# The fourth window's last head pair through a DMA, and the whole order searched anew

## The chip, the cores and the metric

The kernel runs on one core of one Trainium2 chip. The metric is the device time of one execution in microseconds (us); lower is better. The time given for the kernel before is the median of three runs.

## The reference

For 4 batches, 8 heads, 768 tokens and a head dimension of 48, a gated linear attention keeps a 48x48 state per head, and a feed-forward network (FFN) with an ELU between its two matrices follows:

```python
for t in range(S):
    state = alpha[:, :, t, :, None] * state + np.einsum('bhd,bhe->bhde', k[:, :, t], v[:, :, t])
    y[:, :, t] = np.einsum('bhd,bhde->bhe', q[:, :, t], state)
...
x = attn_out.transpose(0, 2, 1, 3).reshape(B * S, H * D)      # 3072 x 384
h = x @ w_in                                                  # 384 x 2048
g = np.where(h > 0.0, h, np.exp(np.minimum(h, 0.0)) - 1.0)
return g @ w_out                                              # 2048 x 384
```

The two weight matrices come as 64-bit floats. The result is fp32.

## The kernel before

**Windows.** Each batch is cut into 6 windows (spans) of 128 tokens, 24 windows in all. A window holds all 8 heads as 4 head pairs; the FFN's input has 3 x 128 rows, so the first three pairs lie in it as they are computed and the fourth has to be spread over the free rows of the other three. The recurrence is done in chunks of 64 tokens by matmuls. Steps are written as tokens, name.window:

- L loads a window's k, q and alpha in one transfer (LA and LB: alpha alone, and k or q alone, for the first two windows); LV loads v. All input transfers, weight transfers and most outputs are issued by SP's queue, in order.
- SC is the scan of alpha on VectorE (DVE, L300), LN and EX are Ln and Exp on ScalarE (ACT, L312 and L318), KA, KB and KC scale k (L326, L331, L336; KA and KB on DVE or GpSimd (POOL), by the tables KAV and KBV), SQ scales q (L354, L357, table SQV), PC is a check sum on ACT (L341).
- TP transposes k on TensorE (PE, L379) and KN copies it out on ACT (L409); for later windows T does both on DVE (L389).
- S makes the scores (L444, L428), MK masks them on DVE (L461, L456), U, UA, UB, UC carry the state (L491, L473; L508 to L541).
- Y (L552 for windows 0 to 4, L557 behind) makes the window's output, XH copies it to the FFN's input xt as the high part (L620, L621), XL makes the low part (L643 and L647 on DVE; XP and a copy on ACT for windows 0 to 2).

**The fourth head pair.** For windows below DIRECT, YL makes that pair's output alone (L552, tile yl), Y3 copies it (L594), and the first matmuls of Y spread it over the free rows by a selection matrix (L606, 6 matmuls, 12 records). For the other windows Y makes all four pairs, XH and XL write the fourth pair's high and low parts into a tile of its own, and XD moves them into xt by two DMAs on SP (L654):

```python
for a in range(2):
    nc.sync.dma_start(out=x[64 * a + D:64 * a + 64]..., in_=y3[64 * a:64 * a + D]...)
```

**Weights.** F loads one piece of 768 KB. KW (ACT, L687), DA (L703) and DB (L708, both DVE) make fp32 words of it, WH (ACT, L735) the high part and WL (L755, DVE or POOL by the table WLV) the low part. LC, CA and CB check the weights. F, KW, DA, DB, WH and WL of all 16 pieces end at about 100 us.

**FFN.** There are 9 blocks: three of 256 tokens (2 windows each, 8 steps j), six of 384 (3 windows, 16 steps). A.b.j makes h in a PSUM bank (L787), RA, RB (ACT, L796, L801) and RC (DVE, L807) the ELU, GH (ACT, L813) and GL (L820, DVE or POOL by the table GQ) its high and low parts, O.b.j multiplies by the second matrix (L836), Z copies the result out (L846) and sends it (L849). RC also frees h's bank. The tiles r, gh, gl and ot come from a ring of 11 buffers.

**The order.** A string of some 1,640 tokens (ORDER) gives one order for the whole program; each engine takes its instructions in that order and waits for what it needs. BANKS and SLOTS are strings that give each PSUM tile its bank and each ring tile its buffer. X.n tokens and WARM put dummy matmuls on PE (L209, tiles xf and wp).

Of the kernel before, what the change touches and what calls it, by code (L numbers as in the profile page):

```python
# [61 lines left out]
YL.1 Y3.1 XP.0 Y.1 WH.2 XL.0 WH.0 F.6 MK.2 YL.2 KA.3 KB.3 KC.3 TP.3 WL.0 XH.1 KN.3 XP.1 XL.1 S.3 WL.2 F.4 KW.2 F.3
DA.2 Y3.2 LV.3 A.0.0 KW.1.1 RA.0.0 DA.1.1 F.7 F.1 DB.2 WH.6 WL.6 UB.2 DB.1.1 Y.2 XH.2 U.3 L.5 MK.3 F.5 UC.2 UA.3 PC.3
A.0.1 YL.3 WH.4 WL.4 KW.1.0 DA.1.0 RB.0.0 RC.0.0 DB.1.0 SC.5 RA.0.1 GH.0.0 UB.3 GL.0.0 L.4 RB.0.1 Y3.3 F.8 WH.1 A.0.3
RA.0.3 WL.1 WH.3 WL.3 XP.2 XL.2 F.10 RB.0.3 RC.0.1 Y.3 XH.3 LV.7 RC.0.3 UC.3 XL.3 KW.3 A.0.2 DA.3 SC.4 LN.5 A.1.1 DB.3
RA.0.2 RB.0.2 RA.1.1 EX.5 KA.5 O.0.0 RB.1.1 A.1.0 KW.4 RC.0.2 RC.1.1 RA.1.0 RB.1.0 GH.0.1 GL.0.1 GH.0.2 LN.4 F.12 DA.4
DB.4 WH.10 RC.1.0 GH.1.0 LC.1 A.1.3 KB.5 GL.1.0 WH.7 WH.8 WL.7 GH.1.1 F.9 GL.0.2 GL.1.1 A.1.2 O.0.1 RA.1.2 RB.1.2
WL.10 EX.4 O.1.0 CA.1 RC.1.2 KA.4 WH.5 WL.8 O.1.1 GH.1.2 WL.5 RA.1.3 RB.1.3 GL.1.2 A.1.5 RC.1.3 GH.0.3 F.14 ZV.6 KW.6
DA.6 CB.1 F.11 A.0.4 O.1.2 RA.0.4 RB.0.4 A.0.5 RA.1.5 O.0.2 KB.4 DB.6 WH.14 GL.0.3 SQ.4 KC.4 S.4 WH.12 RB.1.5 RA.0.5
RC.0.4 L.6 KC.5 RC.1.5 DA.5 GH.0.4 KW.5 LV.6 MK.4 TP.4 RB.0.5 GH.1.5 RC.0.5 KN.4 TP.5 KN.5 LC.3 DB.5 GH.1.3 O.0.3 PC.4  # L70
SQ.5 CA.3 LV.5 U.5 WH.9 WL.12 S.5 MK.5.1 MK.5.0 A.0.6 WH.11 WL.11 CB.3 RA.0.6 GL.1.3 O.1.3 LV.4 U.4 RB.0.6 RC.0.6 PC.5
# [1026 lines left out]
```

## Time and profile before

| | |
|---|---|
| median of three runs (464.18 to 464.94) | 464.34 us |
| the profiled execution, whole | 465.35 us |
| its span, first to last instruction | 463.5 us |
| mean granted clock of PE | 0.997 |
| PE, DVE, ACT, POOL busy | 98%, 75%, 71%, 46% |

The profile is of one execution. A stretch of the span gives each engine's busy time in us and its count of instructions, PE's granted clock, the share of the DMA engines and what they moved. A line of the timeline gives start, duration, engine, line, operation, and in brackets how long the engine stood still before it and what released it; "x18" merges instructions that follow each other. Matmuls are pipelined, so a merged line is read by start times.

### The profile page before, as it was taken

Reading aid. Unit: us, or ns where it says so; the run is one execution under the profiler, and the core shown is the slowest. Engines: PE = TensorE matmul, PEld = TensorE weight load, DVE = VectorE, ACT = ScalarE, POOL = GpSimd, SP = SyncE. Lnnn points to the kernel's source line nnn. Section 1 sums busy time; section 2 is a strip of 40 time slices with the busy share of each in tenths; the row PEclk is TensorE's granted clock in tenths of the full one; section 3 lists DMA queues with packets and bytes.
Section 4 is the critical chain, followed back from the end, with each engine's and each line's share of the span. In section 5 each row is a group of like instructions: output and inputs, shape, how many; then the busy total and the mean of one; then the engine's idle time right before and its main releaser. Section 6 shows DMA issues by size and latency. Waiting matters only on the chain.

```text
span 463.5 us, 12462 instructions
## 1 busy us (share of the span) xinstructions
PE 456.1 (98%) x4948; PEld 440.3 (95%) x4948; DVE 349.7 (75%) x756; ACT 327.6 (71%) x741; POOL 214.2 (46%) x185
## 2 busy tenths in 40 slices
...
GB/s 256 415 411 286 306 103 159 150 157 104 90 236 10 172 116 178 123 49 138 47 176 139 126 66 179 155 70 154 78 120 35 121 45 52 34 35 85 35 4 57
DMA packets 23715, 61.10 MB, mean 132 GB/s; under 512 B 3040, under 2 KB 10720, under 8 KB 23648
## 3 DMA queue, kind: packets, MB, share of 16 engines
...
q10 hardware_dynamic: 432, 0.59, 0.3%
...
HBM read 53.52 MB, written 4.72 MB: 126 GB/s over the span
## 4 chain that ended last, share of the span: by engine, by line
PE 88%; ACT 5%; DVE 4%; issue 1%; DMA 1%; POOL 0%; DVEq 0%; ACTq 0%; POOLq 0%
PE h L787 38%; PE o L836 38%; PE y L557 4%; PE q L428 2%; PE q L473 2%; PE wp L209 1%; PE y L552 1%; ACT w L735 1%; DVE raw L703 1%; DMA out_dram<-ot 1%; DVE wm L708 1%; ACT gh L813 1%; ACT r L801 1%; ACT r L796 1%; PE y L606 1%
## 5 line engine op out<-in xcount | busy, mean ns | idle before, releaser
L787 PE MATMUL h<-xt,w 128*128 128x384 f32 (+1 forms) x1296 | 200.1, 310 | 0.3 <-DVE r L807 0.3
L787 PEld LDWEIGHTS h<-xt,w 128*128 128x128 f32 x1296 | 190.8, 190 | 1.5 <-DVE r L807 0.4
L836 PE MATMUL o<-w,gh 128*128 128x384 f32 x768 | 188.4, 327 | 0.0
L820 POOL TENSOR_TENSOR gl<-r,gh 128x384 fp32r<-128x384 f32 (+1 forms) x90 | 106.4, 1189 | 158.7 <-ACT gh L813 104.9
L836 PEld LDWEIGHTS o<-w,gh 128*128 128x128 f32 x768 | 134.0, 189 | 0.5
L836 PE MATMUL o<-w,gl 128*128 128x384 f32 x384 | 125.3, 326 | 0.2 <-POOL gl L820 0.2
L796 ACT ACTIVATE r<-h 128x384 f32<-128x384 f32 (+1 forms) x120 | 60.5, 510 | 55.8 <-PE h L787 49.3
L389 DVE STREAM_TRANSPOSE kn<-qka 32x128 f32<-32x128 f32 x256 | 77.5, 303 | 4.2
L807 DVE SCALAR_TENSOR_TENSOR r<-r,h 128x384 f32<-128x384 f32 (+1 forms) x90 | 51.0, 577 | 38.0 <-ACT r L801 31.4
L836 PEld LDWEIGHTS o<-w,gl 128*128 128x128 f32 x384 | 72.6, 189 | 0.6 <-POOL gl L820 0.5
L801 ACT ACTIVATE r<-r 128x384 f32<-128x384 f32 (+1 forms) x120 | 64.1, 543 | 2.0
L813 ACT CAST gh<-r 128x384 fp32r<-128x384 f32 (+1 forms) x90 | 46.4, 528 | 18.6 <-DVE r L807 16.1
L357 POOL TENSOR_TENSOR st<-qka,P 64x512 f32<-64x512 f32 x34 | 43.0, 1265 | 17.4 <-DVE P L300 16.1
L456 DVE TENSOR_TENSOR st<-q,mask 64x256 f32<-64x256 f32 x76 | 32.1, 422 | 9.2 <-PE q L428 6.0
L326 POOL TENSOR_TENSOR qka<-qka,R 128x512 f32<-128x512 f32 x16 | 21.1, 1316 | 29.9 <-ACT R L318 27.8
L807 DVE SCALAR_TENSOR_TENSOR h<-r,h 128x384 f32<-128x384 f32 (+1 forms) x30 | 17.5, 589 | 21.0 <-ACT r L801 20.5
L300 DVE TENSOR_TENSOR_SCAN P<-qka,first 128x516 f32<-128x516 f32 (+1 forms) x25 | 31.0, 1244 | 0.5 <-DMA qka<-in_qka_dram 0.2
L820 DVE TENSOR_TENSOR gl<-h,gh 128x384 fp32r<-128x384 f32 (+1 forms) x30 | 17.3, 582 | 18.2 <-ACT gh L813 7.7
L726 ACT ACTIVATE ck<-ck,lim 128x384 f32<-128x384 int32 x32 | 25.5, 795 | 0.6
L721 ACT ACTIVATE ck<-ck,lim 128x384 int32<-128x384 int8 x32 | 25.3, 792 | 0.0
L312 ACT ACTIVATE R<-P 128x512 f32<-128x512 f32 (+1 forms) x25 | 15.4, 615 | 11.4 <-DVE P L300 11.3
L813 ACT CAST gh<-h 128x384 fp32r<-128x384 f32 (+1 forms) x30 | 14.8, 497 | 8.8 <-DVE h L807 7.2
...
## 6 DMA issues: line engine op xcount, KB each, us to landing
qka<-in_qka_dram SPq DMA_DIRECT2D x18, 770.0 KB, 5.5
...
raw<-in_wgt_dram SPq DMA_DIRECT2D x16, 767.6 KB, 10.5
...
xt<-y SPq DMA_DIRECT2D x40, 48.0 KB, 2.8
```

What stands on the lines that cost most here:

```text
L300: nc.vector.tensor_tensor_scan(out=P[:, n].rearrange("p n w -> p (n w)"), data0=t[:, 2 * NP * W + n.start * AW:2 * NP * W + n.stop * AW], ...
L357: eng(SQV, i).tensor_tensor(out=st[r, a], in0=d["q"][r], in1=pw(i)[r], op=ALU.mult)
L389: nc.vector.transpose(out=kn[32 * t:32 * t + 32, :, 32 * g:32 * g + 32], in_=d["kt"][32 * g:32 * g + 32, :, 32 * t:32 * t + 32])
L456: nc.vector.tensor_tensor(out=d["st"][r, a, :, c * C:(c + 1) * C], in0=d["s4"][a][o], in1=mask[o].unsqueeze(1).broadcast_to([64, NP, C]), ...
L726: nc.scalar.activation(out=t[:, :, 1].bitcast(F32), in_=t[:, :, 0], func=AF.Square, bias=lim[:, 1:2], accum_out=chk_w[:, f:f + 1])
L787: nc.tensor.matmul(h[:, y, :], lhsT=t[:, wi, ws], rhs=x[:, c, xi].rearrange("p (a x) -> p x a", a=2), start=(y == 0 and k == 0), stop=(k = ...
L796: nc.scalar.activation(out=r, in_=d["h"], func=AF.Relu, scale=-1.0)
L801: nc.scalar.activation(out=d["r"], in_=d["r"], func=AF.Exp, scale=-1.0)
L807: nc.vector.scalar_tensor_tensor(out=d["g"], in0=d["r"], scalar=-1.0, in1=d["h"], op0=ALU.add, op1=ALU.max)
L813: nc.scalar.copy(out=gh, in_=d["g"])
L820: q.tensor_tensor(out=gl, in0=d["g"], in1=d["gh"].bitcast(F32), op=ALU.subtract)
L836: nc.tensor.matmul(o[:, 0:DM], lhsT=gt[:, y, ms], rhs=t[:, wi, f * DM:f * DM + DM].rearrange("p (a x) -> p x a", a=2), start=(u == 0 and y ...
```

## The change

DIRECT goes from 4 to 3, so window 3 takes the way of the later windows. WARM goes from 17 to 14, and the fillers from X.4.1, X.4.2, X.2.0 to X.2.1, X.2.2, X.2.0. The five engine tables, ORDER, BANKS and SLOTS are replaced; apart from YL.3, Y3.3, XD.3 and the X tokens ORDER holds the same tokens. The functions are as they were.

```diff
-DIRECT = 4
+DIRECT = 3
...
-WARM = 17
+WARM = 14
...
-WLV, KAV, KBV, SQV = (0, 2, 7, 8, 10, 11, 13, 15),  \
-    (0, 1, 2, 3, 6, 7, 14, 22),  \
-    (0, 1, 2, 3, 4, 7, 11, 22, 23),  \
-    (0, 1, 18, 19)
+WLV, KAV, KBV, SQV = (0, 3, 5, 11, 14),  \
+    (0, 1, 3, 4, 5, 16, 18, 21, 23),  \
+    (0, 1, 2, 5, 6, 16, 17, 20, 21, 22, 23),  \
+    (0, 1, 3, 19)
...
-LA.0.0 SC.0.0 LN.0.0 EX.0.0 LA.0.1 SC.0.1 LB.0.0 LN.0.1 KA.0.0 LV.0.0 KB.0.0 EX.0.1 KC.0.0 TP.0.0 KA.0.1 KB.0.1 KC.0.1
...
+LA.0.0 SC.0.0 X.2.1 X.2.2 LA.0.1 SC.0.1 LN.0.0 EX.0.0 LN.0.1 LA.1 EX.0.1 SC.1 LN.1 LB.0.0 KA.0.1 KA.0.0 KB.0.0 LB.0.1
...
```

GQ holds 90 pairs before and after; 15 of them are exchanged.

DVE at the start of the program, before. The input of window 0 is qka_128, that of window 1 qka_129; L300 is the scan:

```order
L300 SCALAR_TENSOR_TENSOR P<-qka_128,first 128x258 x2
L326 TENSOR_TENSOR qka_128<-qka_128,R 128x256
L331 TENSOR_TENSOR R<-P,R 128x256
L336 SCALAR_TENSOR_TENSOR qka_128<-R,qka_128 128x256
...
L300 SCALAR_TENSOR_TENSOR P<-qka_129,first 128x516
L354 TENSOR_TENSOR st<-qka_129,P 128x512
L354 TENSOR_TENSOR st<-qka_128,P 128x512
L326 TENSOR_TENSOR qka_129<-qka_129,R 128x512
```

The same engine and place after, with window 0 in qka_125 and window 1 in qka_126:

```order
L300 SCALAR_TENSOR_TENSOR P<-qka_125,first 128x258 x2
L300 SCALAR_TENSOR_TENSOR P<-qka_126,first 128x516
L326 TENSOR_TENSOR qka_125<-qka_125,R 128x256 x2
L331 TENSOR_TENSOR R<-P,R 128x256 x2
L336 SCALAR_TENSOR_TENSOR qka_125<-R,qka_125 128x256 x2
L354 TENSOR_TENSOR st<-qka_125,P 128x512
L326 TENSOR_TENSOR qka_126<-qka_126,R 128x512
L331 TENSOR_TENSOR R<-P,R 128x512
```

The scan of window 1 has moved ahead of window 0's KA, KB and KC, and only one SQ stands ahead of window 1's KA.

SP's queue behind the first weight loads, before. L676 are weight loads; L260 loads qka_130 for window 5 and qka_129 for window 4:

```order
L676 DMA raw_508<-in_wgt_dram 128x6141
L676 DMA raw_478<-in_wgt_dram 128x6141
L260 DMA qka_130<-in_qka_dram 128x1540
L676 DMA raw_508<-in_wgt_dram 128x6141
L260 DMA qka_129<-in_qka_dram 128x1540
L676 DMA raw_622<-in_wgt_dram 128x6141 x2
L287 DMA vs_115<-in_vv_dram 64x768
```

After; window 5 is loaded into qka_127, window 4 into qka_126, and L654 is XD.3, which waits for XL.3 on DVE:

```order
L676 DMA raw_587<-in_wgt_dram 128x6141
L260 DMA qka_127<-in_qka_dram 128x1540
L676 DMA raw_597<-in_wgt_dram 128x6141
L676 DMA raw_587<-in_wgt_dram 128x6141
L676 DMA raw_597<-in_wgt_dram 128x6141
L654 DMA xt<-y_636 16x6x128 x2
L260 DMA qka_126<-in_qka_dram 128x1540
L716 DMA ck<-in_wgt_dram 128x768
```

The load for window 4 has moved from ahead of two weight loads to behind XD.3.

PE around window 3's output, before; y_620 and sel are the selection matmuls, w_428 and w_512 the first FFN matrix:

```order
L787 MATMUL h<-xt,w_428 128x256 x18
L552 MATMUL yl<-st,vs_115 64x64 x8
L787 MATMUL h<-xt,w_512 128x256 x18
L625 MATMUL y<-xt,minus 128x384
L606 MATMUL y<-y_620,sel 64x128 x6
L552 MATMUL y<-st,vs_115 48x64 x24
L787 MATMUL h<-xt,w_512 128x256 x18
```

After, with w_427 and w_509 as that matrix and vs_112 as window 3's v:

```order
L787 MATMUL h<-xt,w_427 128x256 x18
L625 MATMUL y<-xt,minus 128x384
L552 MATMUL y<-st,vs_112 64x64 x32
L787 MATMUL h<-xt,w_509 128x256 x36
L836 MATMUL o<-w_601,gh 128x384 x2
```

The separate yl matmuls and the six selection matmuls are gone from this place, and two steps of A stand between Y.3 and the first O.

## Rows read from the trace of the kernel before

**Rows 1.** The page's busy time, share of the span and instructions by engine.

```profile
PE 456.1 (98%) x4948; PEld 440.3 (95%) x4948; DVE 349.7 (75%) x756; ACT 327.6 (71%) x741; POOL 214.2 (46%) x185
```

**Rows 2.** Stretches: length, busy us (instructions) by engine, clock, DMA share, GB/s.

```profile
0.00:5.00 5.00, 3.93 (x10) 1.45 (x11) 2.98 (x13) 2.45 (x5) 2.82 (x13) 1.00 0.56 160
5.00:10.00 5.00, 5.00 (x23) 2.20 (x21) 4.73 (x9) 2.10 (x7) 0.00 (x0) 1.00 0.97 306
10.00:15.00 5.00, 4.40 (x105) 3.54 (x104) 3.96 (x7) 2.14 (x6) 0.14 (x1) 1.00 1.03 418
...
60.00:70.00 10.00, 10.00 (x102) 9.71 (x102) 9.98 (x9) 9.09 (x14) 9.34 (x6) 1.00 0.45 120
```

**Rows 3.** Timeline of PE, 0 to 30 us: start, us, what, count.

```profile
1.07 6.78 PE L209 MATMUL wp<-wz 128*128 128x512 bf16 x17 [1.07 <-DVE wz L184]
...
7.91 1.03 PE L209 MATMUL xf<-wz 128*128 128x512 bf16 x4
...
13.30 0.66 PE L379 MATMUL tp<-ident,qka 128*128 128x128 f32 x4 [0.60 <-DVE qka L336]
...
27.66 2.27 PE L787 MATMUL h<-xt,w 128*128 128x256 f32 x18
```

**Rows 4.** Timeline of DVE and ACT in the same stretch.

```profile
7.61 1.23 DVE L300 TENSOR_TENSOR_SCAN P<-qka,first 128x516 f32<-128x516 f32 x1
...
9.19 0.59 ACT L409 COPY kn<-tp 128x512 f32<-128x512 f32 x1 [0.75 <-PE tp L379]
...
9.68 0.64 ACT L312 ACTIVATE R<-P 128x512 f32<-128x512 f32 x1
...
11.10 0.69 DVE L326 TENSOR_TENSOR qka<-qka,R 128x512 f32<-128x512 f32 x1 [0.94 <-ACT R L318]
...
17.82 0.69 DVE L336 SCALAR_TENSOR_TENSOR qka<-R,qka 128x512 f32<-128x512 f32 x1
```

**Rows 5.** Timeline at the two late starts of PE behind 28 us.

```profile
78.11 1.16 PE L787 MATMUL h<-xt,w 128*128 128x256 f32 x8 [0.29 <-DVE r L807]
...
315.57 0.48 ACT L846 COPY ot<-o 128x384 f32<-128x384 f32 x1
...
319.89 0.51 ACT L813 CAST gh<-r 128x384 fp32r<-128x384 f32 x1 [0.27 <-DMA out_dram<-ot]
...
321.57 0.43 PE L836 MATMUL o<-w,gl 128*128 128x384 f32 x1 [0.19 <-POOL gl L820]
```

**Rows 6.** Chain that ended last, in order of time: start, us, what.

```profile
23.15 0.87 PE y L606 x12
...
37.84 0.80 PE y L606 x12
```

**Rows 7.** A group of instructions, and DMA issues (KB each, median us to landing).

```profile
L643 DVE TENSOR_TENSOR y<-y,y 128x128 fp32r<-128x128 f32 x20 | 5.7, 286 | 4.2 <-ACT xt L621 4.0
...
qka<-in_qka_dram SPq DMA_DIRECT2D x18, 770.0 KB, 5.5
...
raw<-in_wgt_dram SPq DMA_DIRECT2D x16, 767.6 KB, 10.5
...
xt<-y SPq DMA_DIRECT2D x40, 48.0 KB, 2.8
```

**Rows 8.** Timeline: SP's issues, and two steps of DVE.

```profile
23.55 0.33 SPq L260 DMA_DIRECT2D qka<-in_qka_dram  x1
25.45 2.22 SPq L676 DMA_DIRECT2D raw<-in_wgt_dram  x2
...
41.39 0.55 DVE L647 TENSOR_TENSOR xt<-y,xt 128x384 fp32r<-128x384 f32 x1
...
43.08 1.21 DVE L300 TENSOR_TENSOR_SCAN P<-qka,first 128x516 f32<-128x516 f32 x1
```

**Rows 9.** Timeline of PE where it goes from FFN to window work and back.

```profile
314.08 0.33 PE L836 MATMUL o<-w,gl 128*128 128x384 f32 x1
314.34 0.69 PE L428 MATMUL q<-st,qka 48*64 48x64 f32 x32
...
316.40 4.66 PE L787 MATMUL h<-xt,w 128*128 128x384 f32 x27
```

More of the change, by code (lines that the diff above doesn't have):

```diff
@@ L62 @@
[L62 to L71, printed above, removed]
@@ new lines @@
+O.2.3 SC.10 LN.10 EX.10 LV.10 XD.7 RA.2.6 RB.2.6 KA.11 KB.11 GH.2.5 ZV.12 KC.11 PC.11 O.2.4 T.11.0 T.11.2 RC.2.6
+RA.2.7 T.11.1 RB.2.7 KA.10 KB.10 KC.10 GH.2.6 T.10.3 GL.2.5 T.10.1 XD.8 A.3.0 RA.3.0 RC.2.7 A.3.1 A.3.2 LC.4 CA.4
+GL.2.6 SQ.11 RA.3.2 RB.3.2 RC.3.2 O.2.5 L.12 RB.3.0 RC.3.0 LV.11 T.11.3 T.10.2 GH.2.7 GL.2.7 O.2.6 O.2.7 A.3.3 T.10.0
+SQ.10 GH.3.0 GL.3.0 MK.9.0 CB.4 RA.3.1 RB.3.1 SC.12 U.11 S.11 MK.11.0 S.10 Z.2.0 Z.2.1 LN.12 EX.12 RC.3.1 GH.3.1
+MK.11.1 GH.3.2 U.10 RA.3.3 MK.10.1 MK.10.0 RB.3.3 UA.10 A.3.4 RA.3.4 LC.5 RC.3.3 PC.10 KA.12 A.3.14 RA.3.14 UB.10
@@ new lines @@
+RA.5.5 RB.5.5 O.5.1 T.18.0 RC.5.5 A.5.9 RA.5.9 RB.5.9 LC.14 CA.14 KB.19 KC.19 CB.14 MK.17.0 PC.19 T.19.3 O.5.2 T.19.2
+O.5.3 RA.5.10 T.19.0 A.5.7 RA.5.7 RB.5.7 A.5.13 GL.5.4 RC.5.9 O.5.4 RB.5.10 A.5.8 RC.5.10 LC.15 GH.5.5 GL.5.5 GH.5.9
+GL.5.9 GH.5.6 GL.5.6 O.5.5 O.5.6 RA.5.8 RB.5.8 T.18.2 T.18.1 LV.18 U.18 CA.15 CB.15 S.18 LV.19 UA.18 RC.5.8 GH.5.8
+RC.5.7 T.19.1 GH.5.7 Y.17 XH.17 UB.18 UC.18 A.5.15 GH.5.10 RA.5.15 MK.18.0 L.20 GL.5.7 XL.17 RB.5.15 GL.5.8 O.5.7
+O.5.8 MK.18.1 RA.5.13 RB.5.13 RC.5.13 U.19 SC.20 LN.20 GL.5.10 RC.5.15 S.19 A.5.11 UA.19 GH.5.13 MK.19.1 RA.5.11
```

172 lines of the change are left out of this document (86 added, 86 removed), and 8 rows, old and new, of the table GQ.

## The prediction

> **What bounds the kernel now.** I read the busy shares first, then the stretches, then the instructions of TensorE (PE) in order of time. PE is busy for 98% of the span [rows 1], and in a middle stretch such as 60 to 70 us for all of it [rows 2]. So the span is PE's own work plus the few places where PE stands still. There are three kinds. At the start PE runs dummy matmuls or waits for the first windows: one chain of VectorE (DVE), ScalarE (ACT) and transposes leads to the first FFN matmul at 27.66 us [rows 3, 4]. Behind that, two starts of matmuls are late by more than switching costs: at 78.1 us behind a DVE step that frees an accumulator, and at 321.6 us behind a POOL step [rows 5]. Last comes the output of block 8, which the change leaves as it is. The reader is to see that nothing an engine other than PE saves counts by itself: it counts if it removes PE work, shortens the first 27.7 us, or removes a late start. The reverse holds too: DVE is busy 9.98 us of the 10 from 60 to 70 us [rows 2], so a DVE that falls behind there shows up on PE at once.
>
> The sums go against the profiled execution (span 463.5 us, 1.85 us more as a whole, 465.35). That one is 1.01 us above the median of the runs, 464.34, so I apply the differences to the median. A measurement of this kernel tells about 0.2% from no change, 0.93 us.
>
> **Part 1, the head pair of the fourth window.** With DIRECT at 3, window 3 loses YL, Y3 and the 12 records of selection matmuls at the front of Y: 0.80 us [rows 6]. The state and score matmuls of that pair move from YL into Y, one for one (8 and 24 become 32). PE is dense there, so 0.80 us goes in full: **-0.8 us**. What is added lies off PE: one L643 on DVE (0.29 us, [rows 7]), one accumulator read on ACT, and XD.3, two DMAs of 48 KB. The first FFN matmuls on that block (A.1.3) now wait for XD.3. The 40 transfers of this kind took 2.8 us to land in the median [rows 7], but none of them ran before 93 us, when the queues are emptier. I cost XD.3 at nothing: XL.3 ends at 41.94 us at the latest (as before, [rows 8]), by the following sums near 38, and PE has A.0.2, A.0.3 and O.0.0 between Y.3 and A.1.3, some 6 us of work (18 matmuls of A take 2.2 us, [rows 3]). With ACT's steps between Y.3 and XL.3 that covers 2.8 us and two issues with some 1.5 us to spare. If that cover is gone, the price is the rest of the landing, 0 to 2 us.
>
> **Part 2, the start.** Three warm-up matmuls and four fillers go. In the trace PE runs 17 warm-ups for 6.78 us and four fillers for 1.03 us before the second transpose; that transpose lets ACT make kn at 9.19, and only behind it ACT starts the Ln of window 1 at 9.68, although window 1's scan ended at 8.84 [rows 3, 4]. Exp, KA.1 (11.10) and KC.1 follow, and the transposes of window 1 start at 13.30. Now the scan of window 1 stands before KA on DVE, and Ln and Exp before kn on ACT. The scan waits for LA.1, third in SP's order; the third transfer of before was read at 5.09 or earlier. So: scan 5.1 to 6.3, the six half-width steps 2.1 to 2.6 us, SQ.0 0.65, then KA.1 to KC.1 with the 2.14 us that the trace shows from 11.10 to 13.24. That puts window 1's transposes at 11.2 to 11.8, against 13.30: 1.5 to 2.1 us earlier.
>
> Part of it is given back to the loads. In the first 10 us the queues move 160 and 306 GB/s, behind that 418 at a share of 1.03, which is all they have [rows 2]. DA.0.0 now stands ahead of MK.1 on DVE and needs F.0, with 3.74 MB up to its end: 0.80 + 1.53 MB by 10 us, the rest by 13.4, landed at 14 to 15. Then 0.6 (DA), 0.6 (MK.1), 0.35 (UC.1), 1.2 (scan of window 3), 0.7 (KB.2) and 0.7 (KC.2) end at about 19.0, where KC.2 ended at 18.51 before [rows 4]. Window 2's score, transposes, kn (0.59 us, [rows 4]) and state update, some 3.2 us, then put Y.1 at 22.2 against 23.15 [rows 6]. From there the PE steps to A.0.0 are the same, so A.0.0 would start near 26.7 instead of 27.66. ACT takes XH.1, WH.2 and XL.1 in a new order there, so I count **-0.7 us**; the ends are 0 (all returned) and -1.5 (the gain at window 1's transposes kept).
>
> **Part 3, the new order behind it.** PE enters window work from FFN work 28 times instead of 27 (counted in the two orders). One such trip costs, by start times, 0.26 instead of 0.16 us on the way out and about 0.1 us twice on the way back [rows 9]: **+0.25 us**. The late start at 321.6 comes from a buffer that waits for an output transfer: ot at 315.57, the gh that reuses a buffer at 319.89, waiting on that DMA, then gl, then PE [rows 5]. In the new order the buffers of block 5's outputs are reused only after 8.8 to 10.3 us of PE work, against 1.5 to 3.6; the closest such pair is now block 3's, with 2.9 us ahead of the reuse and 4.4 us of PE work behind it. **-0.35 us**. The one at 78.1 I leave as it is. The engine tables move WL of three weight tiles from DVE to POOL and one KA and two KB from POOL to DVE; up to about 78 us DVE loses some 0.9 us net with L643 counted, and POOL, below 80% busy in most of the stretch, takes it. I cost it at nothing; without that cover it is those 0.9 us. For late starts that the trace of before can't show I take **+0.3 us**, between nothing and the 0.8 us that it has in total behind 28 us.
>
> Sum: -0.8 - 0.7 + 0.25 - 0.35 + 0.3 = **-1.3 us**, 463.0. With the far ends: -0.8 - 1.5 + 0.2 - 0.8 = -2.9 and -0.8 + 0.3 + 0.8 = +0.3.
>
> **Rivals.** *The gain is eaten by the full engines (same).* From 30 to 78 us DVE and ACT have hardly any idle time. If PE arrives 1.5 us earlier and they don't, PE waits for accumulators and gl, as it did at 78.1. For it: 9.98 of 10 us [rows 2]. Against it: DVE loses 0.9 us of work, and nowhere in that stretch before did PE wait more than half a microsecond. Then the start's 0.7 and half of part 1 are lost: about 464.1.
>
> *L.4 comes too late (slower).* SP issues in order. Before, it issued L.4 (window 4's inputs) at 23.55, ahead of the last two weight loads, and SC.4 read it at 43.08 without a wait [rows 8]. Now L.4 stands behind XD.3, and XD.3 waits on SP for XL.3. With XL.3 at 38.1, two issues of 0.6 and the 5.5 us that such a load takes [rows 7], L.4 lands at 44 to 45, just when DVE reaches SC.4 by its queue (DA.3, WL.3, KA.5, DB.3, DA.4 behind GL.0.0: about 45). If XL.3 comes at 41.4 as before, it lands at 47 to 48.5, DVE stands 2 to 3 us, and RC.1.0, RC.1.1 and RC.0.2, which free PE's accumulators, stand behind it. PE loses that, less 0.5 us of slack. It decides from an XL.3 later than about 39 us. Time: 464.34 - 0.8 + 2.5 = 466.0. Against it: it needs Y.3 more than 1 us later than my sum.
>
> The loads took 10.5 us from issue to landing in the median where transfers on idle queues took 2.8 [rows 7]. [...]
>
> *The order doesn't do what it says:* the start stays bound by the same chain, and only 0.8 us of PE work goes, less the extra trip: 463.8, within the same class.
>
> **How the numbers follow.** Forecast (faster by more than 0.2%, 461.4 to 463.4): 0.60. Eaten, or only part 1 arrives: 0.28, 463.4 to 465.0. L.4 late: 0.12, 465.3 to 467. The range leaves out most of the last and the very best end: 461.8 to 465.0. Faster 0.60, same 0.28, slower 0.12.
>
> **What would show it.** Right: kn of window 0 near 9 us and window 1's transposes below 12; A.0.0 near 27.0 us; no selection matmul behind window 2; O.0.0 starting near 40.6; gh behind block 5's outputs without a wait on a DMA. Wrong: DVE idle before SC.4 with the DMA as its releaser; PE waiting for xt before A.1.3; more than 1 us in sum of PE waits behind 28 us; A.0.0 at 27.6 or later.

## The result and the profile after

The changed kernel takes 468.52 us (median of five, 467.41 to 469.30) against 464.86 of the kernel before in five runs of its own: ratio 1.0089 (95% interval 1.0078 to 1.0100), 0.9% slower. The forecast was 1.3 us less, and 3.7 us more were measured, so the sum is off by 5 us. The profiled execution is 468.88 us, with a span of 467.1.

The page's busy time of after, to be held against [rows 1]:

```profile
PE 454.4 (97%) x4929; PEld 438.8 (94%) x4929; DVE 347.9 (74%) x756; ACT 329.6 (71%) x742; POOL 213.5 (46%) x186
```

PE has less to do, and needs longer. The order of time of PE in the start of after (start, us, what, count, in brackets the idle time before and what ended it) stands beside [rows 3]:

```profile
11.93 0.66 PE L379 MATMUL tp<-ident,qka 128*128 128x128 f32 x4
12.51 1.15 PE L444 MATMUL sc<-st,qka 48*64 48x64 f32 x32
13.59 1.27 PE L491 MATMUL u<-vs,kn 128*64 128x48 f32 x32
15.78 0.58 PE L552 MATMUL yl<-st,vs 64*64 64x64 f32 x12 [0.92 <-issue]
...
20.93 1.15 PE L444 MATMUL sc<-st,qka 48*64 48x64 f32 x32 [0.75 <-DMA raw<-in_wgt_dram]
22.01 0.66 PE L379 MATMUL tp<-ident,qka 128*128 128x128 f32 x4
23.34 0.68 PE L473 MATMUL q<-vs,kn 64*64 64x48 f32 x32 [0.68 <-ACT kn L409]
23.84 0.84 PE L606 MATMUL y<-y,sel 64*64 64x128 f32 x12
24.51 1.07 PE L552 MATMUL y<-st,vs 48*48 48x64 f32 x29
27.03 0.67 PE L552 MATMUL y<-st,vs 48*48 48x64 f32 x17 [1.45 <-issue]
```

The same steps in before, as far as [rows 3] does not have them:

```profile
19.86 1.15 PE L444 MATMUL sc<-st,qka 48*64 48x64 f32 x32
21.27 0.68 PE L473 MATMUL q<-vs,kn 64*64 64x48 f32 x32 [0.27 <-DMA vs<-in_vv_dram]
23.85 1.56 PE L552 MATMUL y<-st,vs 48*48 48x64 f32 x48
```

The transposes of window 1 (11.93) are 1.4 us earlier than before (13.30), nearly as forecast; in three more profiles with the same opening (a_xd16, a_direct4, a_l5 below) they come at 11.14 to 11.62. The first FFN matmul starts at 30.05, 2.4 us later than before (27.66). So from window 1's transposes to A.0.0 it takes 18.12 us, against 14.36 before. By start times PE loses 1.1 us ahead of YL.0 (15.78), 0.35 and 0.85 around XP.0 ahead of window 2's scores (20.93), 0.85 ahead of U.2 (23.34) and 1.6 in the middle of Y.1 (27.03).

VectorE and ScalarE at the places that matter for the first of these waits, in order of time; the first two lines are ScalarE's, the rest VectorE's:

```profile
12.62 0.59 ACT L409 COPY kn<-tp 128x512 f32<-128x512 f32 x1 [2.28 <-PE tp L379]
13.10 0.34 ACT L508 ACTIVATE vs<-u 128x192 f32<-128x192 f32 x1
...
13.47 0.36 DVE L541 SCALAR_TENSOR_TENSOR vs<-u,P 128x192 f32<-128x192 f32 x1 [1.32 <-ACT vs L508]
13.86 1.23 DVE L300 TENSOR_TENSOR_SCAN P<-qka,first 128x516 f32<-128x516 f32 x1
15.01 0.67 DVE L461 TENSOR_TENSOR st<-sc,mask 128x512 f32<-128x512 f32 x1
15.59 1.19 DVE L703 TENSOR_SCALAR raw<-raw 128x768 int32<-128x768 int32 x1
16.70 0.68 DVE L461 TENSOR_TENSOR st<-sc,mask 128x512 f32<-128x512 f32 x1
17.74 0.36 DVE L541 SCALAR_TENSOR_TENSOR vs<-u,P 128x192 f32<-128x192 f32 x1 [0.36 <-ACT vs L508]
18.13 1.23 DVE L300 TENSOR_TENSOR_SCAN P<-qka,first 128x516 f32<-128x516 f32 x1
19.28 0.67 DVE L331 TENSOR_TENSOR R<-P,R 128x512 f32<-128x512 f32 x1
19.98 0.69 DVE L336 SCALAR_TENSOR_TENSOR qka<-R,qka 128x512 f32<-128x512 f32 x1
```

ScalarE in before:

```profile
13.61 0.33 ACT L508 ACTIVATE vs<-u 128x192 f32<-128x192 f32 x1 [2.54 <-DVE vs L541]
13.99 0.58 ACT L409 COPY kn<-tp 128x512 f32<-128x512 f32 x1
```

In after PE has made window 0's u by 12.0. ScalarE could read it then (L508, UA.0), but KN.1 (L409) stands ahead of UA.0 in the new order, where UA.0 stood first before, so UA.0 runs at 13.10, and VectorE, whose UC.0 (L541) needs it, stands still for 1.32 us with SC.2 and MK.0 behind it. YL.0 waits for that MK.0 (15.01). Further down, KC.2 of window 2 (L336) ends at 20.67, where it ended at 18.51 before [rows 4]: besides that wait, SC.3 (18.13) now stands ahead of KB.2 and KC.2. Window 2's scores start 0.26 us behind it. (The bracket at 20.93 names a weight load; the program also waits there for this VectorE step, and the runs below that move the step move the scores.)

The 1.6 us in Y.1 are of another kind. Each L552 matmul of the program leaves two records (24 of them the 48 of before at 23.85), and 29 stand ahead of the gap: it lies inside one matmul, where the program has no wait, and no engine ends a step there. What lands just before is a packet of the queue that the profile labels instruction, by what follows a block of PE's own program. The DMA queues of after between 24.5 and 25.7 us, and over the whole span:

```profile
q8 instruction: 1, 0.02, 5.8%
...
q8 instruction: 41, 0.67, 0.6%
```

That is 41 packets of 16 KB (packets as the profile counts them); this one, the second, was moved from 24.56 to 25.67. They are PE's by what follows: PE's stops below lie 256 of its records apart, each behind one such packet, and only PE has the instructions for 41 such blocks (4,929 matmuls and as many weight loads are 38.5 times 256; VectorE has 756 instructions). Between 18 and 24.5 us the queues were full (q1, the data's, at a share of 101.5%) and no packet of q8 came.

Behind the start, from the first FFN matmul to the last matmul, after takes 431.8 us and before 430.9. The two late starts of [rows 5] are gone (0.45 and 0.35 us by start times), and new ones stand at 55.45 (0.4), 181.76 (0.4) and 297.66 (0.9). The last one, on PE and on SP (SP's line is the issue of XD.17 and XD.16):

```profile
296.26 1.73 PE L787 MATMUL h<-xt,w 128*128 128x384 f32 x9
298.73 2.51 PE L787 MATMUL h<-xt,w 128*128 128x384 f32 x14 [0.74 <-DMA xt<-y]
...
293.34 3.40 SPq L654 DMA_DIRECT2D xt<-y  x4
```

XD.17 and XD.16 are issued one behind the other, right ahead of block 6's first matmuls, though XL.16 was done at 271.2, some 23 us earlier.

### The profile page after: what moved, and what is told of

The parts are those of the page before. It is cut to its first block, busy times and chain, and to the rows that moved or that the text cites. A ratio compares the mean times of both kernels' runs of the same rounds, so it can differ in the third digit from the quotient of the medians.

```text
span 467.1 us, 12449 instructions
## 1 busy us (share of the span) xinstructions
PE 454.4 (97%) x4929; PEld 438.8 (94%) x4929; DVE 347.9 (74%) x756; ACT 329.6 (71%) x742; POOL 213.5 (46%) x186
## 4 chain that ended last, share of the span: by engine, by line
PE 89%; ACT 5%; DMA 2%; issue 1%; SPq 1%; DVE 1%; ACTq 0%
PE o L836 38%; PE h L787 38%; PE y L557 4%; PE q L473 2%; PE q L428 2%; DMA raw<-in_wgt_dram 2%; PE wp L209 1%; PE y L552 1%; PE sc L444 1%; ACT raw L687 1%; PE tp L379 1%; ACT w L735 1%; ACT gh L813 1%; DMA xt<-y 1%; ACT r L796 1%
## 5 line engine op out<-in xcount | busy, mean ns | idle before, releaser
L787 PE MATMUL h<-xt,w 128*128 128x384 f32 (+1 forms) x1296 | 200.5, 310 | 1.0 <-DMA xt<-y 0.7
L787 PEld LDWEIGHTS h<-xt,w 128*128 128x128 f32 x1296 | 190.5, 190 | 2.6 <-DVE st L456 1.0
L820 POOL TENSOR_TENSOR gl<-r,gh 128x384 fp32r<-128x384 f32 (+1 forms) x90 | 101.1, 1130 | 158.3 <-ACT gh L813 101.2
L796 ACT ACTIVATE r<-h 128x384 f32<-128x384 f32 (+1 forms) x120 | 60.8, 511 | 59.4 <-PE h L787 48.0
L357 POOL TENSOR_TENSOR st<-qka,P 64x512 f32<-64x512 f32 x36 | 46.8, 1299 | 8.6 <-DVE P L300 4.8
L326 POOL TENSOR_TENSOR qka<-qka,R 128x512 f32<-128x512 f32 x15 | 19.6, 1304 | 38.5 <-ACT R L318 36.4
L300 DVE TENSOR_TENSOR_SCAN P<-qka,first 128x516 f32<-128x516 f32 (+1 forms) x25 | 30.8, 1234 | 2.6 <-DMA qka<-in_qka_dram 2.2
L807 DVE SCALAR_TENSOR_TENSOR h<-r,h 128x384 f32<-128x384 f32 (+1 forms) x30 | 17.8, 595 | 17.4 <-ACT r L801 17.1
L820 DVE TENSOR_TENSOR gl<-h,gh 128x384 fp32r<-128x384 f32 (+1 forms) x30 | 17.4, 587 | 12.6 <-ACT gh L813 10.7
L726 ACT ACTIVATE ck<-ck,lim 128x384 f32<-128x384 int32 x32 | 25.8, 807 | 0.5
L557 PE MATMUL y<-st,vs 128*64 128x64 f32 x608 | 20.1, 224 | 0.0
```

Source lines behind the costliest of these rows:

```text
L300: nc.vector.tensor_tensor_scan(out=P[:, n].rearrange("p n w -> p (n w)"), data0=t[:, 2 * NP * W + n.start * AW:2 * NP * W + n.stop * AW], ...
L357: eng(SQV, i).tensor_tensor(out=st[r, a], in0=d["q"][r], in1=pw(i)[r], op=ALU.mult)
L557: nc.tensor.matmul(out[64 * a:64 * a + m], lhsT=lhs(i, c, a)[:, n * D:n * D + m], rhs=d["st"][:, a, n, c * C:(c + 1) * C], start=start, st ...
L787: nc.tensor.matmul(h[:, y, :], lhsT=t[:, wi, ws], rhs=x[:, c, xi].rearrange("p (a x) -> p x a", a=2), start=(y == 0 and k == 0), stop=(k = ...
L796: nc.scalar.activation(out=r, in_=d["h"], func=AF.Relu, scale=-1.0)
L807: nc.vector.scalar_tensor_tensor(out=d["g"], in0=d["r"], scalar=-1.0, in1=d["h"], op0=ALU.add, op1=ALU.max)
```

## The experiments

Theory after this reading: the loss is not in part 1 but in the order. In the start three things stand in a row: UA.0 behind KN.1, SC.3 ahead of KC.2, and a block of PE's instructions that comes late through full DMA queues. Behind it come new waits, the transfers of XD.16 the largest. Rivals: part 1 costs what it saves; the gap in Y.1 belongs to an operand; all that is late later is late because of the start.

All times are medians, each beside runs of before on the same chip. Those medians differ (464.07 to 464.86), so ratios are compared. Where the executions of a kernel fall in two groups, as in a_fill, the ratio differs from the quotient of the two medians. Runs named b_ start from the kernel before, the others from the changed kernel; "UA.0 moved" is UA.0 ahead of KN.1 on ScalarE.

| run | edit | us | ratio to before (95%) |
|---|---|---|---|
| changed kernel | none | 468.52 | 1.0089 (1.0078 to 1.0100) |
| b_direct3 | part 1 alone | 469.96 | 1.0125 (1.0108 to 1.0142) |
| b_cover | part 1 with cover | 466.08 | 1.0033 (1.0023 to 1.0042) |
| a_direct4 | part 1 undone | 469.37 | 1.0108 (1.0090 to 1.0125) |
| u_direct4 | part 1 undone, UA.0 moved | 468.73 | 1.0101 (1.0083 to 1.0119) |
| splice | start of before | 466.26 | 1.0047 (1.0034 to 1.0059) |
| a_fill | 40 tiny dummies | 468.11 | 1.0065 (1.0044 to 1.0086) |
| a_l5 | L.5 earlier on SP | 468.48 | 1.0094 (1.0080 to 1.0108) |
| a_busy | a_fill, wide dummies | 467.27 | 1.0060 (1.0043 to 1.0076) |
| a_ua0_only | UA.0 moved | 467.41 | 1.0065 (1.0052 to 1.0078) |
| a_ua0 | a_fill, UA.0 moved | 465.90 | 1.0029 (1.0012 to 1.0046) |
| a_chain | SC.3 moved | 468.10 | 1.0075 (1.0060 to 1.0090) |
| a_busy_chain | a_busy, SC.3 moved | 467.59 | 1.0068 (1.0049 to 1.0086) |
| a_ua0_chain | a_ua0, SC.3 moved | 468.09 | 1.0080 (1.0067 to 1.0094) |
| a_xd16 | XD.16 earlier | 467.61 | 1.0077 (1.0062 to 1.0091) |
| a_best1 | several | 465.94 | 1.0034 (1.0021 to 1.0047) |
| a_best2 | several | 465.67 | 1.0038 (1.0020 to 1.0056) |
| a_best3 | several | 464.42 | 0.9999 (0.9990 to 1.0009) |

**Part 1 in the order of before.** First alone:

```diff
-DIRECT = 4
+DIRECT = 3
-... A.0.1 YL.3 ... RB.0.1 Y3.3 F.8 ... UC.3 XL.3 KW.3 ...
+... A.0.1 ... RB.0.1 F.8 ... UC.3 XL.3 XD.3 KW.3 ...
```

> Part 1 alone in the order of before: DIRECT 3, YL.3 and Y3.3 left out, XD.3 right behind XL.3. Theory (part 1 as in the prediction, the loss of the changed kernel lies in the new order): 12 records of selection matmuls go, 0.8 us less PE work, A.1.3 does not wait for the two transfers; 464.1 us against 464.86 of before. Rival (the transfer or the wider read-out of window 3 costs what the selection saved, and is part of the loss): 464.9 or more, with PE waiting for xt before A.1.3 or DVE waiting in front of SC.4.

469.96 us. PE at block 1's first matmul, and SP (the lines of this kernel stand nine higher, L796 is L787):

```profile
38.45 2.27 PE L796 MATMUL h<-xt,w 128*128 128x256 f32 x18
44.76 3.66 PE L796 MATMUL h<-xt,w 128*128 128x256 f32 x18 [4.04 <-DMA xt<-y]
...
41.59 1.39 SPq L663 DMA_DIRECT2D xt<-y  x2
```

The rival's mechanism: A.1.1 follows A.0.2 there, and the two transfers, issued to 42.98, let it start at 44.76. The price of the missing cover is 4.2 us, twice the most that the prediction gave it, since XH.3 and XL.3 are late too. Right behind that gap the granted clock fell as well (length, busy us of PE, PEld, DVE, ACT, POOL, granted clock, DMA share, GB/s):

```profile
45.34:48.75 3.41, 3.41 (x17) 3.41 (x17) 0.47 (x1) 0.29 (x1) 0.00 (x0) 0.50 0.99 349
```

So the 5.8 us of this run hold the gap and a half clock behind it. Then with Y.3 and O.0.0 moved ahead:

```diff
-... WH.1 A.0.3 RA.0.3 WL.1 WH.3 WL.3 ... Y.3 XH.3 ... XL.3 ... LN.5 A.1.1 ... KA.5 O.0.0 ...
+... WH.1 Y.3 XH.3 A.0.3 RA.0.3 WL.1 WH.3 WL.3 XL.3 XD.3 ... LN.5 O.0.0 A.1.1 ... KA.5 ...
```

> Part 1 in the order of before as in the run with DIRECT 3, but with cover for the transfer: Y.3 and XH.3 ahead of A.0.3, XL.3 and XD.3 right behind WL.3, O.0.0 ahead of A.1.1, so that A.0.3, A.0.2 and O.0.0 (6.4 us of PE work) stand between Y.3 and the first matmul on block 1. Theory (part 1 saves 0.8 us when the transfer is covered; the 4.2 us gap at 40.45 of that run was the missing cover): no gap before A.1.1, 463.4. Rival (XL.3 or XD.3 comes late all the same): a gap of 1 us or more there, 464.5 or more.

466.08: no gap ahead of A.1.1, but not the forecast gain. New or longer late starts took it: 0.5 us inside Y.3 (35.86), 0.9 at 51.45, 0.8 at 78.26, 0.6 at 99.91 and at 322.72. PE that comes earlier meets engines that do not.

**Part 1 undone in the changed order.**

```diff
-DIRECT = 3
+DIRECT = 4
-... XH.2 UA.3 RC.0.0 A.0.1 ... GL.0.1 XD.3 A.1.3 ...
+... XH.2 UA.3 RC.0.0 YL.3 Y3.3 A.0.1 ... GL.0.1 A.1.3 ...
```

> Part 1 alone undone in the changed kernel: DIRECT 4, YL.3 and Y3.3 ahead of A.0.1, XD.3 left out. Theory (part 1 saves the 0.8 us of selection matmuls there, since A.0.2, A.0.3 and O.0.0 cover XD.3; the loss is all in the order): 0.8 us more than the changed kernel, 469.3, with the same gaps in the start. Rival (the transfer costs what it saves): 468.5 or less.

469.37, 0.9 us more by the ratios, with intervals that overlap. And YL.3 brought a wait of 1.0 us of its own at 34.13, while the gap in Y.1 was 0.35 shorter, so I undid it once more with UA.0 moved (below) and YL.3 Y3.3 behind A.0.1, to be held against a_ua0_only:

> The changed kernel with UA.0 ahead of KN.1, and part 1 undone: DIRECT 4, YL.3 and Y3.3 right behind A.0.1 as in the order of before, XD.3 left out. Compare with the run that has UA.0 ahead of KN.1 alone (467.41). Theory (part 1 saves 0.8 us of matmuls, its transfer is covered): 468.2. Rival (what it saves is lost in the waits behind, since VectorE and ScalarE don't get done earlier): 467.4.

468.73 against 467.41, ratios 1.0101 and 1.0065, 1.7 us, intervals apart. Both signs agree: part 1 saves something in the new order, 0.9 to 1.7 us (forecast 0.8; the size is no better known), and the order alone costs more than the change as a whole.

**Start or rest.** All tokens up to A.0.0 in the order of before (with its warm-ups and engine choices), the new order behind, DIRECT 3:

> The start of before (all tokens up to A.0.0 in its order, with its warm-ups, fillers and engine choices, without YL.3 and Y3.3) and the order of the changed kernel behind it, DIRECT 3. Theory (the start is the larger half of the loss: A.0.0 at 30.05 against 27.66, 2.4 us; the rest, 1.2 us in spite of 0.8 us less matmul work, lies in the waits behind): A.0.0 near 27.6, time 466.0. Rival (all of the loss comes from the start, and what is late behind it is late because of it): 463.4 to 463.9. Rival (the loss is behind the start): 468.

466.26. A.0.0 comes at 27.25, and the waits at 52.6, 178.9 and 294.8 (0.4, 0.4, 0.8) are there all the same. So about 2 us of the loss are the start's, and the rest is not its consequence: with 0.8 us less matmul work the new order is still 2 us behind.

**The block of instructions.** Dummies ahead of everything shift the program against the blocks:

```diff
+        for _ in range(40 if k == 2 else 0): nc.tensor.matmul(t[0:32, 0:8], lhsT=wz[:, 0:32], rhs=wz[:, 0:8], start=True, stop=True)
```

> The changed kernel with 40 tiny matmuls (8 columns each) put behind the filler at 6.5 us, where PE stands still until 8.66 us. They add 80 instructions to PE's program ahead of everything. Theory 1 (PE runs out of instructions in the middle of Y.1: the gap of 1.66 us at 25.37 lies between the two passes of one matmul, and the second block of PE's instructions was moved at 24.56 to 25.67): the request for that block comes 40 matmuls earlier, the block lands before PE needs it, the gap goes, A.0.0 starts near 28.5 instead of 30.05, and the time is 467.0. Should it still run out, the gap stands 40 matmuls earlier in the program, in U.2 or the selection of Y.1. Rival (the gap belongs to an operand of Y.1): it stays behind the 29th record of Y.1 with about its length, and the time is 468.5.

The gap in Y.1 is gone, and its rival fits no longer. The time fell to 465.7 and 466.1 in two executions only; in the others and in the profiled one it is 468.1 to 468.4. The profiled one shows why: in place of the gap, the clock. Stretches of a_fill (length, busy us of PE, PEld, DVE, ACT, POOL, granted clock, DMA share, GB/s):

```profile
20.00:24.00 4.00, 2.45 (x54) 1.92 (x57) 3.97 (x7) 3.27 (x8) 0.32 (x1) 1.00 1.00 412
24.00:27.40 3.40, 3.40 (x73) 3.39 (x65) 3.19 (x6) 0.83 (x1) 1.51 (x1) 0.50 1.04 427
27.40:31.00 3.60, 3.60 (x81) 3.28 (x78) 1.76 (x4) 2.84 (x6) 1.29 (x1) 1.00 1.01 410
```

Ahead of the 0.50 PE was busy 2.45 of 4 us. From U.2 to the transposes of window 3 it takes 4.77 us here (23.73 to 28.50); the same matmuls take 3.14 at 1.00 in the last run below (21.91 to 25.05). The fall costs 1.6 us, as much as the gap. Next the block was brought forward without touching PE's program, by one move on SP. L.5 is issued no earlier than 22.43 there, so three weight loads, and not one, are held back behind it:

```diff
-... WL.2 F.1 KW.2 ... F.7 L.5 SC.5 ...
+... WL.2 L.5 F.1 KW.2 ... F.7 SC.5 ...
```

> The changed kernel with nothing but L.5 ahead of F.1 on SP (as the order of before has one of these weight loads behind L.5): 0.77 MB less are queued between 18 and 22.7 us, and PE's program has the same instructions at the same places. Theory (the block of PE's instructions is late because the DMA queues are full): it is moved 1 to 2 us earlier than 24.56, the gap in Y.1 shrinks from 1.66 us to 0.7 or less, A.0.0 comes as much earlier; 467.5. Rival (the request itself is late or the gap is something else): packet and gap stay, 468.4.

The packet came at 21.88 instead of 24.56 and the gap went. The time stayed. In the profiled execution the clock fell from 23.3 to 26.7 and took the gain back:

```profile
19.30:23.30 4.00, 2.44 (x53) 1.90 (x57) 3.97 (x7) 3.27 (x8) 0.31 (x1) 1.00 0.69 279
23.30:26.70 3.40, 3.40 (x75) 3.39 (x66) 3.19 (x6) 0.83 (x1) 1.52 (x1) 0.50 0.93 320
```

For the other executions of a_l5 that is not shown: one with a mean clock of 1.000 took 468.06.

The place of the stop follows from counting PE's records in the trace (matmuls, weight loads and PE's waits) from the start. Over all 19 traces every stretch above 0.1 us behind the first transposes in which PE stood still without a wait in the program lies behind 449, 705, 961 or 1,217 records, which is 256 apart each time. With the packet that ended last, the stops and the passages stand like this (us):

| run | records ahead | packet | PE's last start | goes on | behind the packet's end |
|---|---|---|---|---|---|
| u_direct4 | 449 | 15.48 to 16.57 | 17.4 | 17.85 | 1.28 |
| a_ua0_only | 449 | 15.33 to 16.44 | 17.0 | 17.73 | 1.28 |
| a_best1 | 449 | 15.17 to 16.29 | 17.2 | 17.64 | 1.35 |
| after | 705 | 24.56 to 25.67 | 25.4 | 27.03 | 1.36 |
| a_xd16 | 705 | 23.74 to 24.86 | 24.6 | 26.24 | 1.38 |
| a_direct4 | 705 | 23.86 to 24.98 | 24.9 | 26.20 | 1.22 |
| u_direct4 | 705 | 22.94 to 24.03 | 23.9 | 25.30 | 1.27 |
| a_ua0_only | 705 | 22.74 to 23.84 | 23.5 | 25.30 | 1.46 |
| a_busy | 961 | 28.20 to 29.30 | 29.7 | 30.58 | 1.28 |
| u_direct4 | 961 | 29.17 to 30.26 | 31.3 | 31.72 | 1.45 |
| b_cover | 1,217 | 33.72 to 34.81 | 35.9 | 36.39 | 1.58 |
| before | 705 | 21.92 to 23.02 | no stop | passes at 24.52 | 1.50 |
| a_l5 | 705 | 21.88 to 22.97 | no stop | passes at 26.53 | 3.55 |

PE goes on 1.2 to 1.6 us behind the end of the packet. Before passed the same count 1.50 us behind it: it had nothing to spare.

Why the packet was so late in the changed kernel is only half shown. Measured from PE's passing of the place 256 records earlier it came 5.7 us behind in after (18.85 to 24.56) and 3.3 in a_l5 (18.55 to 21.88), so the order of the loads matters. But it came 3.0 us behind in before (18.92 to 21.92) and 3.05 in a_fill (17.92 to 20.97), with the DMA engines as full between these times (a share of 1.02 and 1.03, after 1.01). So full queues alone do not make the 5.7 us; what else does stays open.

**The clock.** On top of a_fill, wide dummy matmuls in the three waits:

```diff
-... YL.0 ... S.2 ... U.2 ...
+... X.4.0 YL.0 ... X.4.0 S.2 ... X.3.0 U.2 ...
```

> The changed kernel with the 40 tiny matmuls of the run before and 4, 4 and 3 wide dummy matmuls (0.21 us each) put into the three waits of PE ahead of YL.0, S.2 and U.2, where PE stands still for 1.1, 1.2 and 0.9 us. They add no work behind the start. Theory (with PE standing still in these waits its granted clock falls to half for 3.4 us just where Y.1 runs, in some executions; the rows of the run with the tiny matmuls show 0.50 from 24.0 to 27.4 us): the clock stays at 1.00 there and all runs lie near the two fast ones of that run, 465.9. Rival (the fall has nothing to do with these waits): runs stay split between about 466 and 468.

The mean granted clock is 0.998 to 1.000 in all six executions (a_fill: 0.994 to 0.998). A mean is to be read with care: in the profiled execution of before 0.997 comes from 0.50 behind 461 us, after the last matmul, and costs nothing. A fall of 3.4 us in the start, as a_fill shows it, takes 0.0037 off (half of 3.4 in some 465), so by this estimate means of 0.998 and more hold none, and 0.996 or 0.997 alone proves none. With the waits filled the clock held, so PE's standing still has to do with the fall. It does not decide it alone: the profiled execution of after has the same waits and the stop in Y.1 as well, and kept its clock:

```profile
20.00:24.00 4.00, 2.57 (x73) 2.12 (x74) 4.00 (x6) 2.89 (x7) 0.70 (x1) 1.00 1.01 419
24.00:27.40 3.40, 1.95 (x58) 1.80 (x53) 3.18 (x6) 0.83 (x1) 1.13 (x1) 1.00 1.03 417
```

What decides between one execution and another is open. The time of a_busy, 466.7 to 467.8, is above the 465.9: the dummies delay S.2 by 0.4 us, and PE now runs out ahead of the third block, 0.8 us at 29.70.

**VectorE's and ScalarE's order.**

```diff
-... KC.1 TP.1 KN.1 UA.0 LB.1.1 ...
+... KC.1 TP.1 UA.0 KN.1 LB.1.1 ...
```

> The changed kernel with nothing but UA.0 ahead of KN.1 on ScalarE; no tiny matmuls. Theory (both causes stand in a row, and the block of instructions comes when the DMA queues let it): window 2's scores come 1.0 us earlier, but PE runs out at the same place of its program, 29 records into Y.1, for longer than 1.66 us; A.0.0 gains at most 0.5 us; 468.0 to 468.4. Rival (the request for the block moves with PE, so the 1.0 us arrives in full): 467.4.

467.41: 1.1 us gained, the rival's number (the interval just touches that of the changed kernel). From window 1's transposes the scores of window 2 come 1.0 us earlier and A.0.0 0.9. The gap in Y.1 stays at the same record and is 0.1 us longer; the packet moved with PE. VectorE of this run, against the rows at 13.47 and 13.86 above:

```profile
11.62 0.36 DVE L541 SCALAR_TENSOR_TENSOR vs<-u,P 128x192 f32<-128x192 f32 x1 [0.32 <-ACT vs L508]
12.01 1.23 DVE L300 TENSOR_TENSOR_SCAN P<-qka,first 128x516 f32<-128x516 f32 x1
```

With the 40 dummies as well:

> The changed kernel with the 40 tiny matmuls, and UA.0 ahead of KN.1 on ScalarE as in the order of before. In the changed kernel VectorE stands still from 12.15 to 13.47 us because UC.0 waits for UA.0, which stands behind KN.1 on ScalarE although its input is there at 12.0. Theory (this is the first link of the slower start): UC.0, SC.2 and MK.0 come 1.0 us earlier, PE's 1.1 us wait ahead of YL.0 goes, and from the transposes of window 1 to A.0.0 it takes 15.4 us instead of 18.1 (about 16.5 with the tiny matmuls at full clock); time 465.0, and no fall of the clock. Rival (DA.0.0, which needs the first weight load, holds VectorE there anyway): the wait moves behind YL.0 and the time stays at 465.9 to 468.

465.90. The executions reach from 464.2, which is before's time, at a mean clock of 0.999, to 468.1 at 0.991; those at 0.998 and above alone still reach from 464.2 to 465.7. The two edits together give 2.6 us (2.8 by the ratios). The second link, SC.3 behind KC.2, was tried three times, with LN.3 and EX.3 placed differently:

```diff
-... SQ.2 SC.3 LN.3 EX.3 YL.1 ... KC.2 S.2 ...
+... SQ.2 YL.1 ... KC.2 SC.3 LN.3 EX.3 S.2 ...
```

> The changed kernel with SC.3, LN.3 and EX.3 moved behind KC.2, so that VectorE's scan of window 3 no longer stands ahead of the two steps that window 2 waits for. KC.2 should end at 19.4 instead of 20.67 and the score matmuls of window 2 start at 20.2 instead of 20.93. Theory 1 (PE's instruction block, which comes when it comes, sets the end of the start): the gap in Y.1 gets longer by what the chain gains, A.0.0 stays near 30.0, time 468.5. Rival (the chain on VectorE sets it): A.0.0 near 29.3, time 467.8.

> The same, and on VectorE SC.3 behind KC.2, with LN.3, EX.3 and KA.3 behind KN.2, so that nothing of window 3 stands ahead of window 2's chain on VectorE and ScalarE. Theory (VectorE's chain SC.3, KB.2, KC.2 sets when S.2 and U.2 start): KC.2 ends 1.2 us earlier, U.2 starts 0.7 to 1.2 us earlier against window 1's transposes, time 465.0 to 465.3. Rival (the next wait, window 3's steps that are now later, takes it): A.0.0 stays, 465.9.

> The same, with SC.3 behind KC.2 on VectorE and LN.3, EX.3, KA.3, KB.3 behind Y3.1, so that nothing of window 3 stands ahead of window 2. Theory (SC.3 ahead of KB.2 and KC.2 is the second link): score matmuls of window 2 another 0.7 to 1.2 us earlier, 14.4 us from window 1's transposes to A.0.0, time 464.0 to 464.4. Rival (window 3's steps, now later, make TP.3 late and take it back): 465.0.

In a_chain KC.2 came 1.2 us earlier and the scores 0.8 us, measured from window 1's transposes (8.19 against 9.00); then KN.2 waited behind LN.3 and EX.3 on ScalarE, and PE stood 1.5 us for it; the gap in Y.1 is gone there, but the clock of the profiled execution stood at 0.50 from 22.4 to 25.8, and A.0.0 gained 0.25 us. In a_busy_chain Y3.1 was behind them and Y.1 waited 0.8 us. In a_ua0_chain window 3 itself came late; on POOL and PE:

```profile
24.22 1.18 POOL L331 TENSOR_TENSOR R<-P,R 128x512 f32<-128x512 f32 x1 [7.27 <-DVE qka L326]
...
26.23 0.63 PE L379 MATMUL tp<-ident,qka 128*128 128x128 f32 x4 [1.00 <-PE yl L552]
```

(PE waits for KC.3, which stands behind that POOL step on VectorE.) In the start this took 0.7 us: from window 1's transposes to A.0.0 16.09 us, against 15.40 in a_best2, which has the same start without the move and kept its clock. But a_ua0_chain as a whole is 2.2 us slower than a_ua0, which no rival had. From A.0.0 to the last matmul it takes 434.8 us against 431.6: PE waits 0.8 us in Y.3 at 36.4, 1.2 for a POOL step (WL, L755) at 42.9 and 0.8 for gl at 56.0. So the link exists (KC.2 moved the scores), and undoing it moves the wait one window on or behind the start. Of the three times only a_chain's 468.10 lies near a forecast.

**The late transfer, and all of it together.** XD.16 right behind XL.16:

> The changed kernel with XD.16 right behind XL.16, some 25 us earlier on SP, instead of behind XD.17 and right ahead of block 6's first matmul. Theory (the 0.9 us gap at 297.66 is the landing of two pairs of transfers issued one after the other at 293.34 to 296.7): the second pair is gone from there, the first lands by 297.5, the gap shrinks to 0.2 us or less, time 467.7. Rival (what the gap gives back is taken by the next wait, an accumulator that VectorE or ScalarE has not read): 468.4.

The gap at 297.66 is gone; the ratio falls from 1.0089 to 1.0077, about 0.6 us of the 0.8 expected, with intervals that overlap. A gain is not shown: from A.0.0 to the last matmul the profiled execution takes 431.87 us against 431.84, with a new late start of 0.4 us at 244.28 behind a VectorE step, the kind of wait that the rival named. The gap is also absent in the profiles of a_fill, a_busy and a_ua0, which leave XD.16 where it was. The sums:

```
a_best1: UA.0 ahead of KN.1, L.5 ahead of F.1, X.4.0 S.2, X.3.0 U.2, XD.16 behind XL.16
a_best2: 40 dummies, UA.0 ahead of KN.1, XD.16 behind XL.16
a_best3: 32 dummies, UA.0 ahead of KN.1, X.2.0 S.2, X.2.0 U.2, XD.16 behind XL.16, WH.8 WL.8 behind GH.1.0
```

> The changed kernel with UA.0 ahead of KN.1, L.5 ahead of F.1 on SP, 4 and 3 wide dummy matmuls in the waits ahead of S.2 and U.2, and XD.16 right behind XL.16. Theory (these three causes and the late transfer at 297.66 are what the new order loses): no gap in Y.1, granted clock 1.00 through the start in all runs, no gap at 297, 15.4 us from window 1's transposes to A.0.0; 463.6, ahead of before by 0.6 us. Rival (something else of the new order takes it, such as a later block of instructions): 464.5 or more.

> The changed kernel with the 40 tiny matmuls, UA.0 ahead of KN.1 and XD.16 right behind XL.16, no wide dummies. Theory: runs in which the clock holds lie near 463.6 (464.2 of the run without the XD.16 part, less 0.7), those in which it falls near 465.6; the median lies between. Rival: XD.16 gives nothing when the start is faster: 464.2 and 466.3.

> The changed kernel with UA.0 ahead of KN.1, 32 tiny matmuls, 2 and 2 wide dummy matmuls ahead of S.2 and U.2, XD.16 right behind XL.16, and WH.8, WL.8 behind GH.1.0, which PE waited for at 52.33 and 55.45 in the runs before. Theory: the granted clock holds in all runs, the wait near 52 is gone, all runs at 464.0 to 464.3 (464.5 of the undisturbed runs with 40 tiny matmuls, less up to 0.4): level with before. Rival (the clock falls all the same in some): a split between 464 and 467.

a_best1 keeps its clock and has no gap in Y.1, but S.2 starts 0.5 us later behind the four dummies and PE stands still for 0.9 us ahead of U.3 (30.26). a_best2 reaches from 464.45 at a mean clock of 1.00 to 468.2 at 0.991. a_best3 holds the clock in all eleven executions (0.998 to 1.000) and lies at 464.42, ratio 0.9999: PE in its start runs

```profile
11.49 0.65 PE L379 MATMUL tp<-ident,qka 128*128 128x128 f32 x4
...
19.50 1.15 PE L444 MATMUL sc<-st,qka 48*64 48x64 f32 x32 [0.31 <-DVE qka L336]
...
21.91 0.68 PE L473 MATMUL q<-vs,kn 64*64 64x48 f32 x32 [0.24 <-ACT kn L409]
...
23.08 1.56 PE L552 MATMUL y<-st,vs 48*48 48x64 f32 x48
```

So the whole loss is given back by these edits together, and no version is ahead of before. What each of the five gives in a_best3 was not taken apart.

## Why the prediction was wrong

**What bounds the kernel.** Right in the main: what was found is PE standing still, or at half clock, in the start and at single late starts.

**Part 1.** Right in its sign and in the cover. XD.3 is issued from 41.59, A.1.3 starts at 45.62 without a wait, and undoing part 1 costs 0.9 to 1.7 us.

**Part 2, the step that failed.** The first half held: window 1's transposes at 11.93 against the forecast 11.2 to 11.8. Behind them the prediction had two steps, and each failed by 1.7 us.

The first is the end of KC.2, "at about 19.0"; it was 20.67. The prediction added durations from VectorE's queue as if nothing in it waited. It had the order and did not read ScalarE's beside VectorE's: UA.0 behind KN.1 held up VectorE, and DA.0.0 started at 15.59 where the sum needs about 14.9 (moving UA.0 gave 1.0 us). Of the rest, 0.6 is DA.0.0 itself, which took 1.19 us instead of 0.6 next to a POOL step of 15.18 to 16.36 (the neighbourhood is seen, the cause was not tried), and 0.36 is a second wait of UC.1 for ScalarE.

From there the 3.2 us to Y.1 were right (20.67 to 23.84). The second failure is "the PE steps to A.0.0 are the same": from 23.84 to 30.05 it is 6.2 us, against 4.5 before (23.15 to 27.66). The 1.6 us in which PE's instructions were not there were in no term. Nothing in before's trace shows a price for that; that the DMA share was 1.03 [rows 2] was to be seen, and the prediction drew only on the loads' side of it. Forecast −0.7, measured +2.4.

**Part 3.** The −0.35 came: block 5's reuse no longer waits. The extra trip was put at 0.25, where the three pieces named for it add up to 0.3. The new late starts were taken at 0.3, "between nothing and the 0.8"; three of them alone are 1.7 us. That bound is the other step of the prediction that failed: what a different order can make late is not limited by what the old order had late. Beside the 1.7 new, the 0.8 gone and part 1's 0.8, some 0.85 us are left to make the 0.95 that this part measures (431.84 against 430.89); the 0.25 for the extra trip is among them, the others are small pieces that I did not trace.

The sum: start 3.1 us off, the rest 1.55, and 0.3 behind the last matmul.

**The rivals.** "Eaten by the full engines" is what b_cover and the late starts show, but it was priced as a lost gain, not as a loss. The rival of L.4 did not come, though its condition did: XL.3 ended at 41.5, later than the 39 us at which it was to decide, and L.4 was issued at 43.02. But VectorE, busy throughout, reached SC.4 only at 48.96 and not at "about 45", and no transfer held it. None of the three rivals ended as high as 468.5.

**Still open.** Whether the clock also fell in the timed executions of the changed kernel: its profiled one kept 1.00 and lost to the gap, and the four others have mean clocks of 0.991 to 0.996. The end of the program took 0.003 off in the profiled execution of before (0.997). The 0.991 is too low for that alone; the 0.996, 0.001 below it, decides nothing.
